# Scores of a chunked attention on TensorE: 12 products with a half-zero key operand replaced by 24 products over 64 rows each

## The chip, the core and the metric

The kernel runs on one core of a Trainium2 chip as one launch. The metric is the device time of that launch in microseconds (us). Engines are named as in the profile: PE is TensorE's matrix multiplication, PEld its weight loads, DVE is VectorE, ACT is ScalarE, POOL is GpSimd, SP is the queue from which nearly all transfers are issued.

## What is computed

Attention inside chunks of 64 tokens, then two MLPs, one after the other:

```python
q_c, k_c, v_c = ...            # B=8, H=8, S=576, D=64, in 9 chunks of 64 tokens
scores = scale * np.matmul(q_c, k_c.transpose(0, 1, 2, 4, 3))
scores = scores - np.max(scores, axis=-1, keepdims=True)
attn = np.exp(scores)
attn = attn / (np.sum(attn, axis=-1, keepdims=True) + 1e-09)
out = np.matmul(attn, v_c)
x = out.transpose(0, 2, 1, 3).reshape(4608, 512)
h = x @ w_in                                            # 512 -> 2048
x = (np.maximum(h, 0) + np.log1p(np.exp(-np.abs(h)))) @ w_out
h = np.maximum(np.maximum(x @ w1, x @ w2), x @ w3)      # 512 -> 768
out = h @ w_out2
```

## The kernel before

Tokens go in 9 blocks of 512. Products use a 4-byte type (`fp32r`) in which one product is not exact enough, so an operand is split into a high and a low part, and `PASS` runs three products (high by high, high by low, low by high) into one accumulator.

Attention works in 36 tiles: a tile is one block of 512 tokens by two heads, so that the two heads' 64 features fill 128 partitions. The first 8 tiles take a start-up path (`attention_first`). The other 28 take `attention`, which is spread between the steps of the first MLP: a step is `mlp1`, 12 products of 512 columns into `ph` (L743) and 12 into `acc` (L763).

One tile of `attention`: q and k are loaded and transposed on DVE (L633, L638) so that partitions 0 to 63 hold the features of one head and 64 to 127 those of the other. q is split into `Qh` (high and low, 128 x 512 each). k is split by `fill` into `kb`, two tiles of 128 x 1024 that hold, for each group of 32 tokens, the rows of head 0 with zeros beneath and then the rows of head 1 with zeros above; the zeros were written once by POOL (`zeros`, L1088). One product over all 128 rows, 128 query tokens by 256 key columns (L667), then gives the scores of both heads, which stand side by side in one accumulator bank. There are 4 groups of 128 tokens and 3 passes, so 12 products to a tile. The scores (`aps`, two banks, one buffer that the second product of the attention and other steps share) are copied to `p` by ACT and DVE in two copies of 64 x 512 (`copy_op`, L249 and L251), then come softmax on DVE and ACT, a transpose by way of DRAM, `fill` for the probabilities (`pb`) and 24 products with v (L720: weights of 64 columns, 128 moving columns).

The order of work on every engine comes from `Plan`: each operation carries a cost by engine (the scores `{"P": 1.31}`) and a due time, and a greedy list schedule fixes engine and order before the program is written. Buffers come from named pools (`places`); pool `z` has 4 slots of 128 x 2 x 512, which two key tiles and two probability tiles hold from the ninth tile on.

The second MLP follows (`mlp2`: L913, products of 256 columns, and L1024).

Of the kernel before, what the change touches and what calls it, by code (L numbers as in the profile page):

```python
# [20 lines left out]
P = 128  # L21
# [36 lines left out]
class Plan:  # L58
# [6 lines left out]
    def op(self, engs, fn, r=(), w=(), alloc=(), hold=(), after=(), due=None, lat=0.0, move=0.0):  # L65
        o = Op()
        o.move = move
        o.follow = o.start = None
        o.engs, o.fn, o.due, o.lat, o.allocs = engs, fn, due, lat, list(alloc)
        deps = dict.fromkeys(after)  # L70
        bufs = dict.fromkeys(o.allocs + list(hold))
        for item in r:
            b, key = item if isinstance(item, tuple) else (item, None)
            deps.update(dict.fromkeys(b.writers[key] if key in b.writers and key is not None else sum(b.writers.values(), [])))
            bufs[b] = None
        for item in w:
            b, key = item if isinstance(item, tuple) else (item, None)
            if key is None:
                deps.update(dict.fromkeys(sum(b.writers.values(), []) + sum(b.readers.values(), [])))
            else:  # L80
                deps.update(dict.fromkeys(b.writers.get(key, []) + b.readers.get(key, []) + b.readers.get(None, [])))
            bufs[b] = None
        for item in r:
            b, key = item if isinstance(item, tuple) else (item, None)
            b.readers.setdefault(key, []).append(o)
        for item in w:
            b, key = item if isinstance(item, tuple) else (item, None)
            b.writers[key] = [o]
        for b in bufs:
            if b.first is None:  # L90
                b.first = o
            else:
                deps[b.first] = None
        o.deps = list(deps)
        o.bufs = list(bufs)
        for b in o.bufs:
            b.uses += 1
        o.n = len(self.ops)
        self.ops.append(o)
        return o  # L100
# [78 lines left out]
def tile_kernel(ctx: ExitStack, tc: tile.TileContext, q, k, v, w_in, w_out, w1, w2, w3, wo2, out):  # L179
# [20 lines left out]
    def mem(kind, n, shape, dt, where=pool):  # L200
# [3 lines left out]

        "w": list(range(32)),
        "x": list(range(32, 40)),
        "z": list(range(40, 44)),
        "qh": [44],
        "vh": [45],
        "load": list(range(3)),  # L210
# [413 lines left out]
    def attention(t, after=()):  # L624
# [1 line left out]
        due_s, due_p = due_v - 2.0 * STEP, due_v - 1.4 * STEP  # L626
        Rq, Rk, Rv, Qh, Vh = Buf("rq"), Buf("rk"), Buf("rv"), slot("qh"), slot("vh")
        qT, kT = Buf("tmp"), Buf("tmp")
        kb, pb = big["k"], big["p"]
        loads(load_32(t, q, lambda: Rq.t), Rq, "q", 2.2, [Rq], after=after)  # L630
        loads(load_32(t, k, lambda: Rk.t), Rk, "k", 2.2, [Rk], after=after)
        loads(load_v(t, lambda: Rv.t), Rv, "v", 1.6, [Rv], after=after)
# [2 lines left out]
        tt_op(lambda: Qh.t[:, 1], lambda: qT.t, lambda: Qh.t[:, 0].bitcast(F32), ALU.subtract, [qT, (Qh, "h")], [(Qh, "l")])  # L635
        copy_op(lambda: Vh.t[:, 0], lambda: Rv.t, [Rv], [(Vh, "h")], alloc=[Vh])
        tt_op(lambda: Vh.t[:, 1], lambda: Rv.t, lambda: Vh.t[:, 0].bitcast(F32), ALU.subtract, [Rv, (Vh, "h")], [(Vh, "l")])
        op({"D": 0.69}, lambda e: nc.vector.transpose(kT.t, Rk.t), r=[Rk], w=[kT], alloc=[kT], after=last_p[-1:])  # L638

        def fill(dst, src, s):  # L640
            view = lambda l, e, r: dst[l].t.rearrange("p (u e s) -> p u e s", e=2, s=s)[r, :, e, :]
# [15 lines left out]
                )  # L657

        parts = lambda z: [(l, e) for l in z for e in range(2)]
        fill(kb, kT, 32)  # L660
        sc = Buf("aps")

        def do_s(e):
            o = sc.t.rearrange("p u (h f) -> p (u h) f", h=2)
            for h in range(HP):
                for n, (l, m) in enumerate(PASS):
                    nc.tensor.matmul(  # L667
                        o[:, h],
                        Qh.t[:, l, h * P:(h + 1) * P],
                        kb[m].t[:, 2 * h * P:2 * (h + 1) * P],  # L670
                        start=(n == 0),
                        stop=(n == 2),
                    )

        o = op({"P": 1.31}, do_s, r=[Qh] + parts(kb), w=[sc], alloc=[sc], after=last_t[-1:], due=due_s)
        last_s.append(o)

        pbuf = Buf("p")
        for c, r in enumerate(ROWS):
            copy_op(  # L680
                lambda r=r: pbuf.t[r].rearrange("p (a h i) -> p h a i", a=4, h=HP),
                lambda r=r, c=c: sc.t.rearrange("p u (h c a i) -> p (u h) c a i", c=2, a=4, i=32)[r, :, c],
                [sc],
                [(pbuf, c)],
                psum=True,
                alloc=[pbuf] if c == 0 else [],
            )
        softmax(
            pbuf,
            lambda red: pbuf.t.rearrange("p (b u i) -> p u b i" if red else "p (b u i) -> p b u i", b=2, i=32),  # L690
# [394 lines left out]
    def zeros(name, after):  # L1085
        big[name] = [slot("z", shape=[P, 2 * TB]) for _ in range(2)]
        for z in big[name]:
            op({"G": 0.9}, lambda e, z=z: nc.gpsimd.memset(z.t.bitcast(F32), 0.0), w=[(z, "z")], alloc=[z], after=after)  # L1088
# [12 lines left out]
    for n, (b, j, first, last) in enumerate(steps):  # L1101
        if n >= NJ and n % (NJ // HP) == 0:
            t = HP + n // (NJ // HP)
            if t < NTILE:
                if t == 2 * HP:
                    zeros("k", [done])
                    zeros("p", [done])
                attention(t, [first_loads[min(t, 11)]])
        h = mlp1(b, j, first, last)
        if b >= 2 and j in (0, 3, 6, 9) and len(store_early) < 4 * NJ2:  # L1110
            early(len(store_early), T0 + STEP * (n + 7), [h])
            store_early.append(h)
        if (b, j) == (NB - 1, 0):
            begun = [h]
# [40 lines left out]
```

## Time and profile before

| what | value |
|---|---|
| median of 3 runs (lowest to highest) | 1552.93 us (1551.62 to 1554.88) |
| the profiled execution's own time | 1553.11 us |
| its span, first to last instruction | 1551.4 us |
| PE busy | 1524.7 us, 98% |
| PEld busy | 1318.1 us, 85% |
| DVE busy | 963.3 us, 62% |
| ACT busy | 594.9 us, 38% |
| mean granted TensorE clock | 0.998 |

The span is what the profile covers; the 1.7 us between it and the execution's time lie outside the instructions. Busy time of PE is the time in which at least one product is in flight, and each product's record is longer than the distance to the next one's start. What a block of products costs is therefore read as the distance from its first start to the start of the block behind it.

### The profile page before, as it was taken

How to read it: one execution, taken by the hardware profiler on the slowest of the kernel's cores; microseconds unless marked ns; L12 is line 12 of the kernel's file. 1: busy time of each engine (PE TensorE's matmuls, PEld its weight loads, DVE VectorE, ACT ScalarE, POOL GpSimd, SP SyncE). 2: the span in 40 equal slices, each digit the busy share in tenths (PEclk: the TensorE clock that was granted, in tenths of full speed). 3: DMA queues.
4: the chain of work that ended last, by engine and by line, in shares of the span. 5: the costliest groups of instructions: out<-in, count | busy, mean ns of one | idle time of the engine just before them, and what ended most of it. 6: DMA issues, size and time to landing. Idle time of an engine off the chain costs nothing.

```text
span 1551.4 us, 23011 instructions
## 1 busy us (share of the span) xinstructions
PE 1524.7 (98%) x8930; PEld 1318.1 (85%) x8930; DVE 963.3 (62%) x1834; ACT 594.9 (38%) x1122; POOL 11.7 (1%) x19
## 2 busy tenths in 40 slices
PE   6999999999999999999999999999999999999998
PEld 5777888788888888888888888999999999999997
DVE  7988876866767766767676455553544545545443
ACT  5754344443444334433343343332322323323221
POOL 2000000000000000000000000000000000000000
PEclk9999999999999999999999999999999999999999
DMA  9354134543434425334342221222322122222121
GB/s 251 116 149 122 57 89 105 142 106 85 128 89 103 99 53 140 75 103 102 69 122 69 80 83 48 75 82 71 107 82 82 69 82 102 76 82 102 53 77 69
DMA packets 235214, 147.28 MB, mean 95 GB/s; under 512 B 167009, under 2 KB 202849, under 8 KB 235105
## 3 DMA queue, kind: packets, MB, share of 16 engines
q1 hardware_dynamic: 231904, 144.24, 32.4%
q10 hardware_dynamic: 3200, 1.57, 0.5%
q8 instruction: 70, 1.15, 0.3%
q14 instruction: 40, 0.32, 0.1%
HBM read 109.58 MB, written 36.18 MB: 94 GB/s over the span
## 4 chain that ended last, share of the span: by engine, by line
PE 94%; DVE 4%; DMA 1%; ACT 0%; issue 0%; ACTq 0%; DVEq 0%
PE acc L763 26%; PE ph L743 25%; PE ph L913 13%; PE aps L913 12%; PE acc L1024 10%; DVE tmp L256 3%; PE aps L720 3%; PE aps L667 3%; DMA s<-in_q_dram 1%; PE acc L557 1%; PE acc L606 1%; PE ph L369 1%; PE acc L526 0%; ACT s L249 0%; DVE s L256 0%
## 5 line engine op out<-in xcount | busy, mean ns | idle before, releaser
L763 PE MATMUL acc<-g,s 128*128 128x512 f32 x1728 | 427.7, 397 | 0.0
L743 PE MATMUL ph<-s,s 128*128 128x512 f32 x1728 | 420.0, 392 | 1.2 <-DVE s L256 0.9
L763 PEld LDWEIGHTS acc<-g,s 128*128 128x128 f32 x1728 | 323.4, 188 | 76.9 <-issue 1.0
L743 PEld LDWEIGHTS ph<-s,s 128*128 128x128 f32 x1728 | 321.6, 188 | 72.8 <-DVE s L256 1.2
L256 DVE TENSOR_TENSOR tmp<-aps,tmp 128x256 f32<-128x256 f32 x241 | 99.4, 422 | 280.8 <-PE aps L913 221.5
L913 PE MATMUL ph<-s,s 128*128 128x256 f32 x1944 | 267.6, 283 | 0.0
L913 PEld LDWEIGHTS ph<-s,s 128*128 128x128 f32 x1944 | 251.7, 191 | 4.5
L249 ACT COPY tmp<-ph 128x256 f32<-128x256 f32 x268 | 99.7, 372 | 349.9 <-PE ph L913 348.8
L256 DVE TENSOR_TENSOR g<-tmp,g 128x512 fp32r<-128x512 f32 x198 | 133.9, 687 | 149.9 <-ACT g L249 148.9
L753 ACT ACTIVATE tmp<-ph 128x512 f32<-128x512 f32 x144 | 86.3, 599 | 316.9 <-PE ph L743 312.5
L913 PE MATMUL aps<-s,s 128*128 128x256 f32 x1458 | 203.9, 285 | 3.6
L913 PEld LDWEIGHTS aps<-s,s 128*128 128x128 f32 x1458 | 186.0, 191 | 9.0 <-DVE tmp L256 8.8
L1024 PE MATMUL acc<-s,g 128*128 128x512 f32 x648 | 161.4, 398 | 1.9 <-ACT g L249 1.9
L256 DVE TENSOR_TENSOR s<-tmp,s 64x512 fp32r<-64x512 f32 (+1 forms) x212 | 142.2, 674 | 26.6 <-ACT s L249 22.7
L1024 PEld LDWEIGHTS acc<-s,g 128*128 128x128 f32 x648 | 119.7, 191 | 27.3 <-ACT g L249 2.2
L249 ACT CAST s<-tmp 128x512 fp32r<-128x512 f32 (+2 forms) x190 | 115.1, 609 | 67.4 <-DVE tmp L638 26.6
L249 ACT CAST g<-tmp 128x512 fp32r<-128x512 f32 x192 | 119.1, 620 | 28.3 <-PE acc L763 17.3
L256 DVE TENSOR_TENSOR tmp<-tmp,tmp 128x256 f32<-128x256 f32 (+1 forms) x152 | 83.1, 547 | 3.9
L249 ACT COPY p<-aps 64x512 f32<-64x512 f32 x50 | 29.1, 582 | 68.8 <-PE aps L667 52.8
L249 ACT COPY tmp<-acc 128x512 f32<-128x512 f32 (+1 forms) x66 | 37.3, 588 | 34.2 <-PE acc L1024 17.0
L720 PEld LDWEIGHTS aps<-s,s 128*64 128x64 f32 x672 | 44.5, 135 | 3.8
L667 PEld LDWEIGHTS aps<-s,s 128*128 128x128 f32 x336 | 43.8, 189 | 2.6
(97 smaller groups left out, 957.4 us busy)
## 6 DMA issues: line engine op xcount, KB each, us to landing
s<-wo2d SPq DMA_DIRECT2D x54, 512.0 KB, 3.3
s<-in_moe_w_out_dram SPq DMA_DIRECT2D x22, 512.0 KB, 4.9
x2d<-tmp SPq DMA_DIRECT2D x36, 256.0 KB, 2.8
s<-in_moe_w_dram SPq DMA_DIRECT2D x18, 512.0 KB, 4.2
s<-x2d SPq DMA_DIRECT2D x18, 512.0 KB, 4.6
s<-in_moe_w_in_dram SPq DMA_DIRECT2D x16, 512.0 KB, 4.9
out_dram<-tmp SPq DMA_DIRECT2D x29, 256.0 KB, 4.4
pd<-tmp SPq DMA_DIRECT2D x28, 256.0 KB, 2.1
```

The lines of the kernel that those rows point to most:

```text
L249: nc.scalar.copy(dst(), src())
L256: return op({"D": 0.69 * n}, lambda e: nc.vector.tensor_tensor(dst(), a(), b(), f), r=r, w=w, **kw)
L369: nc.tensor.matmul(o, ident, a.t, start=False, stop=False)
L557: nc.tensor.matmul(o[:, h], qT()[:, h * P:(h + 1) * P], blk[0]()[:, 2 * h:2 * h + 2].rearrange("p u e s -> p (u e s)"), start=True, stop=True,
L606: nc.tensor.matmul(o[:CH, c], rv()[:, c * CH:(c + 1) * CH], blk[1]()[:, c].rearrange("p e s -> p (e s)"), start=True, stop=True,)
L667: nc.tensor.matmul(o[:, h], Qh.t[:, l, h * P:(h + 1) * P], kb[m].t[:, 2 * h * P:2 * (h + 1) * P], start=(n == 0), stop=(n == 2),)
L720: nc.tensor.matmul(o[:CH, c], Vh.t[:, l, c * CH:(c + 1) * CH], z[m][:, c % 2, c // 4, c // 2 % 2], start=(n == 0), stop=(n == 2),)
L743: nc.tensor.matmul(ph.t, w[:, wi, kk * P:(kk + 1) * P], x[kk].t[:, xi], start=(kk == 0 and wi == 0 and xi == 0), stop=(kk == KD - 1 and wi ...
L753: in_line("y", op({"A": 0.6}, lambda e: nc.scalar.activation(l.t, ph.t, AF.Softplus), r=[ph], w=[l], alloc=[l]))
L763: nc.tensor.matmul(acc[m // 2].t[:, m % 2], w[:, wi, m * P:(m + 1) * P], g.t[:, gi, :], start=(first and wi == 0 and gi == 0), stop=(last ...
L913: nc.tensor.matmul(dst(), ws.t[:, wi, col + kk * P:col + (kk + 1) * P], x.t[:, xi, kk * HT:(kk + 1) * HT], start=(first and kk == 0 and wi ...
L1024: nc.tensor.matmul(acc[t // 2].t[:, t % 2], g.t[:, gi, t * P:(t + 1) * P], wo.t[:, wi], start=(j == 0 and wi == 0 and gi == 0), stop=(j == ...
```

## The change

The scores of a tile become 24 products of 64 rows (one head each), 128 query tokens by 128 key columns. Head 0 uses partitions 0 to 63 and writes the first bank of `aps`, head 1 partitions 64 to 127 and the second bank, and the two take turns. k is split like q, dense, into one tile `Kh` of pool `z` (one copy and one subtraction of 128 x 512 in place of two copies and two subtractions of 64 x 512). The key tiles with zeros and their two memsets go, and pool `z` has 3 slots. The scores leave `aps` in four copies of 64 x 256. The cost that the planner has for the scores stays at 1.31.

```diff
-        "z": list(range(40, 44)),
+        "z": list(range(40, 43)),
...
-        kb, pb = big["k"], big["p"]
+        Kh, pb = slot("z"), big["p"]
...
-        op({"D": 0.69}, lambda e: nc.vector.transpose(kT.t, Rk.t), r=[Rk], w=[kT], alloc=[kT], after=last_p[-1:])
+        op({"D": 0.69}, lambda e: nc.vector.transpose(kT.t, Rk.t), r=[Rk], w=[kT], alloc=[kT, Kh], after=last_p[-1:])
+        cut_up(Kh, lambda: kT.t, [kT])
...
-        fill(kb, kT, 32)
         sc = Buf("aps")
 
         def do_s(e):
-            o = sc.t.rearrange("p u (h f) -> p (u h) f", h=2)
+
             for h in range(HP):
+                cols = slice(h * P, (h + 1) * P)
                 for n, (l, m) in enumerate(PASS):
-                    nc.tensor.matmul(
-                        o[:, h],
-                        Qh.t[:, l, h * P:(h + 1) * P],
-                        kb[m].t[:, 2 * h * P:2 * (h + 1) * P],
-                        start=(n == 0),
-                        stop=(n == 2),
-                    )
-
-        o = op({"P": 1.31}, do_s, r=[Qh] + parts(kb), w=[sc], alloc=[sc], after=last_t[-1:], due=due_s)
+                    for u, r in enumerate(ROWS):
+                        nc.tensor.matmul(
+                            sc.t[:, u, cols], Qh.t[r, l, cols], Kh.t[r, m, cols], start=(n == 0), stop=(n == 2)
+                        )
+
+        o = op({"P": 1.31}, do_s, r=[Qh] + parts_of(Kh), w=[sc], alloc=[sc], after=last_t[-1:], due=due_s)
         last_s.append(o)
 
         pbuf = Buf("p")
         for c, r in enumerate(ROWS):
-            copy_op(
-                lambda r=r: pbuf.t[r].rearrange("p (a h i) -> p h a i", a=4, h=HP),
-                lambda r=r, c=c: sc.t.rearrange("p u (h c a i) -> p (u h) c a i", c=2, a=4, i=32)[r, :, c],
-                [sc],
-                [(pbuf, c)],
-                psum=True,
-                alloc=[pbuf] if c == 0 else [],
-            )
+            for u in range(2):
+                copy_op(
+                    lambda r=r, u=u: pbuf.t[r].rearrange("p (b u h i) -> p u h b i", b=2, u=2, h=HP)[:, u],
+                    lambda r=r, c=c, u=u: sc.t.rearrange("p u (h c b i) -> p u h c b i", c=2, b=2, i=32)[r, u, :, c],
+                    [sc],
+                    [(pbuf, (c, u))],
+                    psum=True,
+                    n=0.7,
+                    alloc=[pbuf] if c == 0 and u == 0 else [],
+                )
...
-                    zeros("k", [done])
                     zeros("p", [done])
```

PE before, at the first tile that takes this path. `aps_87` is the accumulator of the scores, `s_95` and `s_99` are the key tiles with zeros (high and low), `s_76` is q; `ph` and `acc` rows belong to the first MLP.

```order
L743 MATMUL ph_86<-s_46_529,s_87_1297 128x512 x3
L667 MATMUL aps_87<-s_95_1485,s_76_1078 128x256
L667 MATMUL aps_87<-s_99_1585,s_76_1078 128x256
L667 MATMUL aps_87<-s_95_1485,s_76_1078 128x256 x2
L667 MATMUL aps_87<-s_99_1585,s_76_1078 128x256
L667 MATMUL aps_87<-s_95_1485,s_76_1078 128x256 x2
L667 MATMUL aps_87<-s_99_1585,s_76_1078 128x256
L667 MATMUL aps_87<-s_95_1485,s_76_1078 128x256 x2
L667 MATMUL aps_87<-s_99_1585,s_76_1078 128x256
L667 MATMUL aps_87<-s_95_1485,s_76_1078 128x256
L763 MATMUL acc_89<-g_65,s_80_1186 128x512 x6
```

PE of the change at the same tile; `s_87_1258` is now k, dense, high and low in one tile.

```order
L743 MATMUL ph_85<-s_46_529,s_65_929 128x512 x3
L763 MATMUL acc_89<-g_63,s_57_801 128x512 x6
L763 MATMUL acc_88<-g_63,s_57_801 128x512 x6
L669 MATMUL aps_87<-s_87_1258,s_76_1078 128x128 x24
L743 MATMUL ph_86<-s_27_348,s_69_979 128x512 x3
```

Twelve products of 256 columns became 24 of 128 columns, and the first tile's block moved several steps forward (it stood behind the step with weights `s_87_1297`, and stands now ahead of the step with `s_69_979`); it no longer waits for POOL's zeros.

DVE of the change at that tile: the transpose of k, the low part of a step's `g`, and the low part of k.

```order
L638 STREAM_TRANSPOSE tmp_73<-rk_76 128x512
L256 TENSOR_TENSOR tmp_74<-tmp_74,s_85_1237 128x512
L256 TENSOR_TENSOR g_64<-tmp_72,g_64 128x512
L256 TENSOR_TENSOR s_87_1258<-tmp_73,s_87_1258 128x512
L312 TENSOR_SCALAR tmp_67<-tmp_67 128x512
```

DVE before at a later tile, where the key operand was filled half by half (`s_95` high, `s_99` low, 64 rows each).

```order
L638 STREAM_TRANSPOSE tmp_71<-rk_76 128x512
L256 TENSOR_TENSOR s_106_1868<-rv_77,s_106_1868 128x512
L251 CAST s_95_1485<-tmp_71 64x16x32
L256 TENSOR_TENSOR s_107_1884<-aps_87,s_107_1884 64x512
L256 TENSOR_TENSOR s_99_1585<-tmp_71,s_95_1485 64x16x32 x2
```

Two subtractions over 64 partitions became one over 128, and the one stands, at the first tile, behind the low part of the step that PE runs just ahead of the scores.

## Rows read from the trace of the kernel before

**Rows 1.** The page: busy time of each engine, and the shares of the chain that ended last by engine and line.

```profile
PE 1524.7 (98%) x8930; PEld 1318.1 (85%) x8930; DVE 963.3 (62%) x1834; ACT 594.9 (38%) x1122; POOL 11.7 (1%) x19
...
PE 94%; DVE 4%; DMA 1%; ACT 0%; issue 0%; ACTq 0%; DVEq 0%
PE acc L763 26%; PE ph L743 25%; PE ph L913 13%; PE aps L913 12%; PE acc L1024 10%; DVE tmp L256 3%; PE aps L720 3%; PE aps L667 3%; DMA s<-in_q_dram 1%; PE acc L557 1%; PE acc L606 1%; PE ph L369 1%; PE acc L526 0%; ACT s L249 0%; DVE s L256 0%
```

**Rows 2.** Busy time of each engine by stretches; the stretch is given in us from the span's start, with its length, then busy us and number of instructions. PEclk is the granted clock.

```profile
core 0: us, PE busy (x) PEld busy (x) DVE busy (x) ACT busy (x) POOL busy (x), PEclk, DMA share, GB/s
120.00:180.00 60.00, 60.00 (x253) 47.25 (x252) 49.16 (x101) 23.62 (x41) 0.96 (x1) 1.00 0.37 106
400.00:600.00 200.00, 200.00 (x1041) 165.94 (x1040) 141.09 (x249) 80.08 (x136) 0.00 (x0) 1.00 0.38 97
600.00:800.00 200.00, 200.00 (x1047) 166.06 (x1045) 139.93 (x247) 80.28 (x136) 0.00 (x0) 1.00 0.38 95
800.00:880.00 80.00, 80.00 (x429) 66.26 (x428) 48.09 (x85) 29.68 (x50) 0.00 (x0) 1.00 0.26 76
```

**Rows 3.** Groups of instructions by line and shape: partitions x elements of the output (and weights' rows*columns for PE), count, then busy us, mean ns of one, and idle time ahead of the group with what ended it.

```profile
L720 PE MATMUL aps<-s,s 128*64 128x128 f32 x672 | 44.9, 223 | 0.0
L720 PEld LDWEIGHTS aps<-s,s 128*64 128x64 f32 x672 | 44.5, 135 | 3.8
L667 PE MATMUL aps<-s,s 128*128 128x256 f32 x336 | 44.5, 282 | 0.0
L667 PEld LDWEIGHTS aps<-s,s 128*128 128x128 f32 x336 | 43.8, 189 | 2.6
```

**Rows 4.** PE in order of time, 215 to 232 us: start, length of the merged piece, line, output, weights' rows*columns, output shape, count.

```profile
217.25 2.97 PE L763 MATMUL acc<-g,s 128*128 128x512 f32 x12
220.06 1.60 PE L720 MATMUL aps<-s,s 128*64 128x128 f32 x24
221.50 2.96 PE L743 MATMUL ph<-s,s 128*128 128x512 f32 x12
224.30 2.98 PE L763 MATMUL acc<-g,s 128*128 128x512 f32 x12
227.11 1.59 PE L667 MATMUL aps<-s,s 128*128 128x256 f32 x12
228.54 2.91 PE L743 MATMUL ph<-s,s 128*128 128x512 f32 x12
```

**Rows 5.** All engines in order of time from 227.08 to 227.12 us, the place where a block of scores begins.

```profile
226.88 0.40 PE L763 MATMUL acc<-g,s 128*128 128x512 f32 x1
226.89 0.61 SPq L408 DMA_DIRECT2D rk<-in_k_dram  x1
227.11 0.28 PE L667 MATMUL aps<-s,s 128*128 128x256 f32 x1
227.12 0.19 PEld L667 LDWEIGHTS aps<-s,s 128*128 128x128 f32 x1
```

**Rows 6.** PEld alone at that place (227.04 to 227.10 us).

```profile
226.88 0.19 PEld L667 LDWEIGHTS aps<-s,s 128*128 128x128 f32 x1
```

**Rows 7.** PEld alone from 221.46 to 221.50 us, where a block with 64 weight columns (L720) ends and a block with 128 (L743) begins.

```profile
221.38 0.13 PEld L720 LDWEIGHTS aps<-s,s 128*64 128x64 f32 x1
221.44 0.19 PEld L743 LDWEIGHTS ph<-s,s 128*128 128x128 f32 x1
```

**Rows 8.** All engines from 221.64 to 221.70 us, just behind that.

```profile
221.44 0.22 PE L720 MATMUL aps<-s,s 128*64 128x128 f32 x1
221.50 0.44 PE L743 MATMUL ph<-s,s 128*128 128x512 f32 x1
221.55 0.19 PEld L743 LDWEIGHTS ph<-s,s 128*128 128x128 f32 x1
```

**Rows 9.** L743 by itself: count, then shortest, median and longest ns.

```profile
L743 PEld LDWEIGHTS ph<-s,s x1728: 186/188/192, 56.3 to 965.2; 128*128 128x128 f32 x192
L743 PE MATMUL ph<-s,s x1728: 387/389/503, 56.3 to 965.4; 128*128 128x512 f32 x192
```

**Rows 10.** Groups on DVE and ACT that the change touches, or that are nearest to what it adds, columns as in the third group.

```profile
L256 DVE TENSOR_TENSOR s<-tmp,s 64x512 fp32r<-64x512 f32 x112 | 76.6, 684 | 10.5 <-ACT s L249 7.7
L256 DVE TENSOR_TENSOR s<-tmp,s 128x512 fp32r<-128x512 f32 x91 | 62.2, 688 | 11.3 <-ACT s L249 10.1
L249 ACT CAST s<-tmp 128x512 fp32r<-128x512 f32 x110 | 67.8, 620 | 35.9 <-DVE tmp L256 20.3 <-DVE tmp L317 15.1
L249 ACT CAST s<-tmp 64x512 fp32r<-64x512 f32 x71 | 43.9, 618 | 30.1 <-DVE tmp L638 26.6 <-POOL s L1088 1.9 <-DMA tmp<-pd 0.7
L249 ACT COPY p<-aps 64x512 f32<-64x512 f32 x50 | 29.1, 582 | 68.8 <-PE aps L667 52.8 <-DVE tmp L256 14.9 <-DVE g L256 0.8
L249 ACT COPY tmp<-ph 128x256 f32<-128x256 f32 x268 | 99.7, 372 | 349.9 <-PE ph L913 348.8
L753 ACT ACTIVATE tmp<-ph 128x512 f32<-128x512 f32 x144 | 86.3, 599 | 316.9 <-PE ph L743 312.5 <-DVE s L326 2.5 <-DMA tmp<-pd 1.5
```

**Rows 11.** Who waited for whom: the waits of PE by themselves, and one of PEld; us in total, times, longest us.

```profile
PE acc L1024 <- ACT g L249: 1.9, 1, 1.9
PE ph L368 <- ACT s L249: 1.2, 1, 1.2
PE ph L743 <- DVE s L256: 0.9, 1, 0.9
...
PEld aps L913 <- DVE tmp L256: 8.8, 26, 0.3
```

## The prediction

> **What bounds the kernel now.** The first view to read is the page's busy time and its last chain: PE is busy for 1524.7 of 1551.4 us, and the chain that ended last is PE for 94% [rows 1]. The stretches say that this holds where the change is made: from 400 to 880 us PE is busy for all of the time at a granted clock of 1.00 (the 2.4 GHz level), while DVE and ACT are busy for about 70% and 40% [rows 2]. PE waits hardly anywhere behind the start-up: its longest waits there are 0.9 to 1.9 us, once each [rows 11]. So in the stage of the change one microsecond of PE is one microsecond of the kernel, and DVE and ACT count only where PE waits for them.
>
> Next, what a block of scores costs PE. Mean durations (282 ns a product) don't say it, since products overlap. Distances between starts do: a block of scores starts at 227.11 and the next block at 228.54, 1.43 us for 12 products of 256 columns, 0.119 us each. The block with v, 24 products of 128 columns with 64 weight columns, goes from 220.06 to 221.50, 1.44 us, 0.060 us each [rows 4]. Count over 12 gives the tiles: 336 / 12 = 28 [rows 3], so all scores cost 28 x 1.43 = 40.0 us, which is the chain's 3% for L667 [rows 1].
>
> Then, what sets these distances. Each product loads its own weights. A load of 128 columns takes 189 ns and one of 64 columns 135 ns [rows 3]: 54 ns for 64 columns, so the streaming part of a full load is about 0.107 us, the rest fixed latency. In steady state it is hidden: the load of the scores' first weights starts at 226.88, together with the product ahead of it, and is long done at 227.11; the second load starts at 227.12, right behind the start of the first product [rows 5, 6]. It shows where the cover is too short. When the block with v ends, the load for L743 starts at 221.44, its product at 221.50, only 0.06 us later, and that product is recorded with 0.44 us where the median is 0.389 [rows 7 to 9]: it stood still for 0.05 us, until its weights were in, 0.11 us after the load began. And the next load starts at 221.55, 0.11 us behind the first, though its product had begun at 221.50. So weights of 128 columns come at one in 0.11 us at best over the same rows. A 256-column product (0.119 us) hides that; a 128-column product (0.060 us) doesn't.
>
> **The change, part by part.** *Scores.* Now 12 loads and 12 x 256 columns; then 24 loads of 64 rows x 128 columns, each with 128 moving columns. The moving columns are 3072 in both, so if nothing ran side by side the columns alone would be 24 x 0.060 = 1.44 us, as now. What can change the time is whether the two heads, in disjoint halves of the array's rows, run side by side, and then the loads decide, since 128 weight columns in 0.11 us stand against 0.060 us of moving columns. All products of the trace, like those in [rows 3, 4], have 128 rows (the first number of their form), so this is bounded from both sides:
> - two loads side by side, and the two products under them: a pair takes one load, 0.107 to 0.119 us (the upper end is what a pair's worth of columns takes now). 12 x 0.110 = 1.32 us, and 1.28 to 1.43 at the ends. The last product's exit is in it, since the following block's first load takes the place of a 13th.
> - loads one behind another: 24 x 0.110 = 2.64 us, 2.57 to 2.86 at the ends.
>
> I take the first, at 0.110: the array already overlaps a load with the product ahead [rows 5], the heads share no partition, and they write different banks. 1.43 - 1.32 = 0.11 us a tile, 28 tiles, **-3.1 us**; ends -4.2 and 0.
>
> The Trainium skill, TensorEngine Tiling (Array Packing), Key Properties, says that different tiles can execute weight loads and products in parallel; no run here shows it yet. By that rule the sum is the one just made. The Trainium skill, TensorE: Matmul & The Clock Gate, LDWEIGHTS, says that a load goes by its columns and not by its rows; by it, too, half the rows don't make a load shorter.
>
> *k.* Out go two casts of 64 x 512 (618 ns on ACT) and two subtractions (684 ns on DVE), in come one cast (620) and one subtraction (688) of 128 x 512 [rows 10], since these take the same over 64 and 128 partitions. That is 0.62 us of ACT and 0.68 of DVE less per tile, hidden under PE's columns: 0. The two memsets on POOL go: 0.
>
> *Copies of the scores.* Two of 64 x 512 at 582 ns become four of 64 x 256; the nearest row is 372 ns for 256 columns, on ACT [rows 10]: 1.49 for 1.16 us. Three of four stand on ACT, so the softmax starts some 0.3 us later at most and `aps` is held so much longer. The next user of `aps` is steps away (a step is 5.6 us): 0.
>
> *Place in the order.* The block of the first tile moves forward, and there its key's low part stands on DVE behind the low part of `g` of the step just done. From the end of that step's `ph`: activation 0.60, two casts of 0.62 on ACT (`g`, then k), one subtraction 0.69 on DVE, 2.5 us and the hand-overs; cover is one block of L763, 2.81 us [rows 4, 10]. Cost 0, at most 0.5 us, once. PE is fully busy there now [rows 2].
>
> *Pool z with 3 slots.* In the second MLP the splits of x draw on it; PE's only repeated wait there is 0.3 us, 26 times, for DVE's sums [rows 11], not for a buffer: 0.
>
> Sum: the profiled execution's 1553.1 us - 3.1 = **1550.0 us**. That execution lies 0.2 us above the median of the runs shown, so it can stand for it. With the ends and 1 us for waits, this case's own range is 1548.5 to 1554.
>
> **The rivals.**
> 1. *Loads one behind another* (slower). Place: the 28 blocks; price 2.64 - 1.43 = +1.21 us a tile, +33.9 us, **1587 us** (2.57 to 2.86: 1585 to 1593). It decides as soon as a pair takes over 0.119 us, that is when the second head's load begins more than 9 ns behind the first's; 18 ns behind is 0.2% of the kernel. For it: loads start 0.11 us apart at 221.44 and 221.55 although the product between was already under way [rows 7, 8]. Against it: those two go to the same rows, where the second has to wait in any case.
> 2. *Loads half covered*: the second load starts some way behind the first (0.13 to 0.17 us a pair, between the two): 1.56 to 2.04 us a block, +0.13 to +0.61, **1557 to 1570 us**. Nothing in the trace sets a point here.
> 3. *Changing the row layout empties the array.* A product's record is 0.40 us long where the distance is 0.23 [rows 4, 5], so about 0.16 us of results would be awaited at the block's start and the load (0.11) laid bare; the same at its end: about 0.5 us a tile, +14 us on the forecast, **1564 us**. Against it: at 217.25 to 224.30 the form of the weights changes from 128 to 64 columns and back, at a cost of those 0.05 us alone [rows 4, 7, 8]. The Trainium skill, TensorEngine Tiling (Array Packing), Key Properties, states the rule that a change of tiling mode drains the engine. By that rule this rival would be the forecast; the trace doesn't bear it out for columns, and has no row for rows.
> 4. *A load of 64 rows takes half as long* and the pairs run at 0.060 us: 0.72 us a block, -0.71 x 28 = -19.9, **1533 us**. No row has a shorter load for other than fewer columns.
> 5. *Nothing runs side by side and loads are hidden nonetheless*: 1.44 us, no change. Rows 7 to 9 speak against it.
>
> **How the numbers follow.** About 0.2% (3.1 us) is what a measurement of this kernel can tell from no change, so the forecast stands at that edge. Chances: forecast 0.42, rival 1 0.30, rival 2 0.14, rival 3 0.06, rival 4 0.07, rival 5 0.01. Faster: 0.45 of the forecast's 0.42 (below 1549.8) and rival 4, 0.26. Same: the rest of the forecast and rival 5, with a little of rival 2's near end, 0.26. Slower: rivals 1, 3 and most of 2, 0.48. For 8 in 10 the range takes the forecast's 0.42 with its low end, rivals 2 and 3 (0.20) and two thirds of rival 1 (0.20): **1548.5 to 1590 us**; rival 4 and the far end of rival 1 are left out.
>
> **What would show it.** In the profile after, the distance from the first score product to the next block, now 1.43 us: 1.3 to 1.4 bears the forecast out, 2.6 or more rival 1, 0.7 rival 4. The starts of the two heads' loads: together, or 0.11 us apart. A gap between the last L763 product and the first score product, and after the last: rival 3. PE idle under 1 us at the first tile, and 100% busy from 400 to 880 us; if PE waits there for `p`, `Kh` or `aps`, the parts that I cost at nothing were wrong. ACT and DVE busy lower by about 8 us (28 x 0.3 us) and 19 us.

## The result, and the profile after

The change makes the kernel slower: 1561.55 us (median of 4 runs, 1561.01 to 1563.39) against 1552.95 us for the kernel before (4 runs), a ratio of 1.0056 with the interval [1.0043, 1.0069]. The forecast was 1550.0 us, a gain of 3 us; the kernel lost 8.6. The time lies inside the range, but the forecast went the wrong way, and the nearest case is rival 3 (1564 us), to which I had given 6 in 100.

The page of the changed kernel, which answers to [rows 1]: busy us, share of the span, instructions.

```profile
PE 1530.9 (98%) x9266; PEld 1315.5 (84%) x9266; DVE 944.2 (61%) x1813; ACT 584.8 (37%) x1143; POOL 9.8 (1%) x17
```

DVE and ACT lost 19.1 and 10.1 us, about as forecast (19 and 8), and it bought nothing: PE is still what bounds the kernel. The stretch of PE in which all changed work lies can be read off the line L743 by itself, which answers to [rows 9]: shortest, median and longest ns, then the first and the last start.

```profile
L743 PE MATMUL ph<-s,s x1728: 387/389/793, 55.5 to 975.3; 128*128 128x512 f32 x192
```

From the first L743 product to the last are 975.3 - 55.5 = 919.8 us; before 965.4 - 56.3 = 909.1 [rows 9]. So **+10.7 us** came into this stage. The stretch ahead of it is 0.8 us shorter and the one behind it 1.3 (1560.0 - 975.3 = 584.7 against 586.0), which makes the 8.6 us between the spans. In the last 14 us the granted clock is 0.97, and was 0.84 in the last 15 us before; neither end holds any work of the scores. Of the change only pool `z` reaches into the second MLP, and PE's one long wait there is 1.9 us as before [rows 11].

**A block of scores.** PE of the changed kernel in order of time, 396 to 405 us, columns as in [rows 4]. In both kernels 23 of the 28 blocks stand like this one, between L763 and L743.

```profile
396.30 2.97 PE L763 MATMUL acc<-g,s 128*128 128x512 f32 x12
399.21 1.56 PE L669 MATMUL aps<-s,s 64*128 64x128 f32 x24
400.69 3.00 PE L743 MATMUL ph<-s,s 128*128 128x512 f32 x12
403.53 1.60 PE L720 MATMUL aps<-s,s 128*64 128x128 f32 x24
```

Read the distances from start to start, and beside them those of the block at 227.11 in [rows 4], which has the same neighbours. The block of scores takes 400.69 - 399.21 = 1.48 us (1.49 at most of the 28), and took 1.43. But its neighbours are longer too: L763 ahead of it takes 2.91 us and took 2.81, L743 behind it 2.84 and took 2.74. All three together take 7.23 us and took 6.98; over the 23 blocks the means are 7.23 and 6.99. That is **0.24 us a tile, 28 x 0.24 = +6.7 us**, of which only 0.06 us a tile shows in the distance that the prediction had named as its test.

Why the neighbours are longer is seen closer by, here at a block with L743 ahead and L763 behind: PE and PEld at the first pair, then at the end (a merged piece is given as start, length and count).

```profile
326.88 0.39 PE L743 MATMUL ph<-s,s 128*128 128x512 f32 x1
327.20 0.19 PEld L669 LDWEIGHTS aps<-s,s 64*128 64x128 f32 x2 [0.35 <-DVE tmp L323]
327.20 0.33 PE L669 MATMUL aps<-s,s 64*128 64x128 f32 x2
...
327.20 0.30 PEld L669 LDWEIGHTS aps<-s,s 64*128 64x128 f32 x4 [0.35 <-DVE tmp L323]
...
328.42 0.19 PEld L669 LDWEIGHTS aps<-s,s 64*128 64x128 f32 x2
...
328.69 0.19 PEld L763 LDWEIGHTS acc<-g,s 128*128 128x128 f32 x1
328.69 0.51 PE L763 MATMUL acc<-g,s 128*128 128x512 f32 x1
```

The pairs do what the forecast said. Two loads together last 0.19 us, as one does; four last 0.30, so the second pair comes 0.11 us behind the first; the two products of the first pair last 0.33 together. What went wrong stands at both ends. Before, the first load of a block ran under the product ahead of it, 0.23 us early [rows 5, 6]. Now the first two loads start only at 327.20, with their own products, and PEld sat idle for 0.35 us ahead of them. At the end, L763's first load starts at 328.69, with its product again and 0.27 us behind the loads ahead of it (328.42), where a pair follows a pair by 0.11. That product is recorded with 0.51 us, against a median of 0.389 for such products [rows 9]: 0.12 us in which it stood still until its weights were in. So at each change between products of 64 and of 128 rows the first load doesn't run under the products ahead but starts with its own product, and that product comes late: 0.32 us behind the last one of L743 (326.88), where such products follow each other by 0.23 us [rows 4]. These are the gaps that the prediction had named as rival 3's sign.

The Trainium skill, TensorEngine Tiling (Array Packing), Key Properties, says that a change of tiling mode drains the engine and that different tiles load and multiply in parallel. For the change of rows this trace agrees with both: the bare loads at 327.20 and 328.69, and the two loads that together last 0.19 us.

**The sixth block.** The rest of the 10.7 us, 4.0, stands at one place. PE after, 279 to 297 us, with two rows of DVE from there; the brackets hold the idle time ahead and what ended it.

```profile
279.32 1.61 PE L720 MATMUL aps<-s,s 128*64 128x128 f32 x24
284.95 1.97 PE L669 MATMUL aps<-s,s 64*128 64x128 f32 x24 [4.02 <-DVE s L256]
286.85 9.59 PE L743 MATMUL ph<-s,s 128*128 128x512 f32 x36
296.28 1.60 PE L720 MATMUL aps<-s,s 128*64 128x128 f32 x24
...
283.50 0.67 DVE L256 TENSOR_TENSOR s<-tmp,s 128x512 fp32r<-128x512 f32 x1
284.21 0.68 DVE L256 TENSOR_TENSOR s<-aps,s 64x512 fp32r<-64x512 f32 x1
```

PE of the kernel before at the same place:

```profile
278.90 1.61 PE L720 MATMUL aps<-s,s 128*64 128x128 f32 x24
280.35 2.28 PE L743 MATMUL ph<-s,s 128*128 128x512 f32 x9
282.94 0.50 PE L743 MATMUL ph<-s,s 128*128 128x512 f32 x1 [0.30 <-ACT s L249]
284.35 6.19 PE L743 MATMUL ph<-s,s 128*128 128x512 f32 x26 [0.91 <-DVE s L256]
290.38 1.60 PE L720 MATMUL aps<-s,s 128*64 128x128 f32 x24
```

Before, three L743 blocks followed L720 there and waited 0.30 and 0.91 us, for the high and the low part of their operand. After, the list schedule put the scores directly behind L720. Both write `aps`, of which there is one buffer, so the scores had to wait until all of L720's result was split out of it: the last subtraction that reads `aps` runs from 284.21 to 284.89, and the scores start at 284.95. The low part of k was in at 284.17, so it was `aps` that they waited for last. The clock then comes on top. Busy time by stretches, columns as in [rows 2]:

```profile
279.30:284.90 5.60, 1.63 (x25) 1.47 (x23) 5.49 (x9) 2.29 (x4) 0.00 (x0) 1.00 0.51 140
284.90:286.90 2.00, 1.95 (x25) 1.83 (x25) 1.91 (x3) 0.00 (x0) 0.00 (x0) 0.76 0.27 57
286.90:288.90 2.00, 2.00 (x7) 1.61 (x6) 1.24 (x3) 1.00 (x3) 0.00 (x0) 0.50 0.56 142
288.90:291.00 2.10, 2.10 (x10) 1.72 (x9) 1.80 (x4) 0.00 (x0) 0.00 (x0) 0.90 0.48 93
```

DVE is busy for 5.49 of the 5.60 us: here it is the bound. Behind the idle time the granted clock falls to 0.76 and then to 0.50 (the 1.2 GHz level), and comes back by 291 us. From L720 at 279.32 to the next at 296.28 are 16.96 us; without waits the same blocks take 1.44 + 0.09 (L720, longer ahead of the scores) + 1.49 + 2.84 + 2 x 2.74 (L743) = 11.34, so 5.6 us are lost. Before it is 290.38 - 278.90 = 11.48 against 1.44 + 2.80 + 2 x 2.74 = 9.72 (2.80 for L743 right behind L720 [rows 4]), 1.8 lost. The net 3.9 us and the 6.7 above make 10.6 of the 10.7 us that the stage lost.

### The profile page after: what moved, and what is told of

It reads as the page before. It is cut to its first block, busy times and chain, and to the rows that moved or that the text cites. A ratio compares the mean times of both kernels' runs of the same rounds, so it can differ in the third digit from the quotient of the medians.

```text
span 1560.0 us, 23657 instructions
## 1 busy us (share of the span) xinstructions
PE 1530.9 (98%) x9266; PEld 1315.5 (84%) x9266; DVE 944.2 (61%) x1813; ACT 584.8 (37%) x1143; POOL 9.8 (1%) x17
## 4 chain that ended last, share of the span: by engine, by line
PE 93%; DVE 4%; DMA 1%; ACT 0%; SPq 0%; issue 0%; ACTq 0%; DVEq 0%
PE ph L743 26%; PE acc L763 25%; PE ph L913 13%; PE aps L913 12%; PE acc L1024 10%; DVE tmp L256 3%; PE aps L669 3%; PE aps L720 2%; DMA s<-in_q_dram 1%; PE acc L557 1%; PE acc L606 1%; PE ph L369 1%; DVE s L256 0%; PE acc L526 0%; ACT s L249 0%
## 5 line engine op out<-in xcount | busy, mean ns | idle before, releaser
L763 PE MATMUL acc<-g,s 128*128 128x512 f32 x1728 | 428.4, 397 | 0.0
L743 PE MATMUL ph<-s,s 128*128 128x512 f32 x1728 | 422.6, 394 | 0.0
L763 PEld LDWEIGHTS acc<-g,s 128*128 128x128 f32 x1728 | 323.3, 188 | 77.4 <-issue 1.0
L743 PEld LDWEIGHTS ph<-s,s 128*128 128x128 f32 x1728 | 322.3, 188 | 72.8 <-issue 0.5
L913 PEld LDWEIGHTS aps<-s,s 128*128 128x128 f32 x1458 | 186.0, 191 | 9.0 <-DVE tmp L256 8.8
L256 DVE TENSOR_TENSOR s<-tmp,s 128x512 fp32r<-128x512 f32 (+2 forms) x184 | 123.0, 673 | 42.2 <-ACT s L249 39.5
L249 ACT CAST s<-tmp 128x512 fp32r<-128x512 f32 (+2 forms) x169 | 101.8, 608 | 58.6 <-DVE tmp L638 24.0
L249 ACT COPY p<-aps 64x256 f32<-64x256 f32 x87 | 28.9, 367 | 78.5 <-PE aps L669 67.1
L669 PEld LDWEIGHTS aps<-s,s 64*128 64x128 f32 x672 | 40.0, 189 | 14.0 <-issue 6.2
L669 PE MATMUL aps<-s,s 64*128 64x128 f32 x672 | 44.0, 278 | 4.0 <-DVE s L256 4.0
```

The lines of the kernel that those rows point to most:

```text
L249: nc.scalar.copy(dst(), src())
L256: return op({"D": 0.69 * n}, lambda e: nc.vector.tensor_tensor(dst(), a(), b(), f), r=r, w=w, **kw)
L669: nc.tensor.matmul(sc.t[:, u, cols], Qh.t[r, l, cols], Kh.t[r, m, cols], start=(n == 0), stop=(n == 2))
L743: nc.tensor.matmul(ph.t, w[:, wi, kk * P:(kk + 1) * P], x[kk].t[:, xi], start=(kk == 0 and wi == 0 and xi == 0), stop=(kk == KD - 1 and wi ...
L763: nc.tensor.matmul(acc[m // 2].t[:, m % 2], w[:, wi, m * P:(m + 1) * P], g.t[:, gi, :], start=(first and wi == 0 and gi == 0), stop=(last ...
L913: nc.tensor.matmul(dst(), ws.t[:, wi, col + kk * P:col + (kk + 1) * P], x.t[:, xi, kk * HT:(kk + 1) * HT], start=(first and kk == 0 and wi ...
```

## The experiments

Each starts from the changed kernel, except the last. The kernel before took 1553.54 us (13 runs) on the chip of the first four, 1551.13 (5 runs) on that of the next four and 1553.55 (13 runs) on that of the last; ratios are to these. To set the runs against each other I use the stage as above, from the first to the last start of the `ph` products: 909.1 us before, 919.8 after. The changed kernel itself was not run again on these chips, so whole times are set against its 1561.55 us with that reserve.

**The place of the sixth block.** The scores of that tile are put behind the first step of a later block.

```diff
-        o = op({"P": 1.31}, do_s, ..., alloc=[sc], after=last_t[-1:], due=due_s)
+        o = op({"P": 1.31}, do_s, ..., alloc=[sc], after=[*last_t[-1:], *behind], due=due_s)
...
-                attention(t, [first_loads[min(t, 11)]])
+                attention(t, [first_loads[min(t, 11)]], [hs[32]] if t == 13 else [])
```

> The changed kernel, with the scores of one tile alone (the sixth of the 28, whose block stood still for 4.0 us at 280.7 us) put behind the first step of the third token block in PE's order. Theory A (the loss is in two parts: about 0.26 us at each of 28 blocks, from changing between products of 128 rows and of 64 rows, and one stall from the new order): the stall goes back to about what the kernel before has there (1.65 us), the 0.7 us of lower clock behind it goes too, so about 3 us less than the changed kernel, 1558.5 us; the 28 blocks keep their 1.49 us. Theory B (the whole loss sits in the 28 blocks and the stall only takes the place of the earlier one): within 0.5 us of 1561.5 us.

Measured: 1560.98 us (1559.75 to 1561.91), 1.0052 [1.0036, 1.0069]. That is 0.6 us below the changed kernel with overlapping ranges: nearer to theory B's number than to A's, and no gain that these runs can tell. PE in order of time:

```profile
285.24 0.50 PE L743 MATMUL ph<-s,s 128*128 128x512 f32 x1 [0.81 <-ACT s L249]
...
292.99 1.60 PE L720 MATMUL aps<-s,s 128*64 128x128 f32 x23 [0.81 <-DVE s L256]
...
387.21 1.56 PE L669 MATMUL aps<-s,s 64*128 64x128 f32 x24 [0.63 <-DVE s L256]
```

The wait of 4.0 us is gone and the clock with it, but the schedule laid smaller waits elsewhere, and the stage is 917.5 us: 2.3 us of the 3.9 came back there, and the stretch ahead of the stage was 1.4 us longer in this execution. The place explains part of the loss and is not the larger part.

**Products over all 128 rows.** The scores become 12 products of 128 rows and 128 columns, which changes what they compute: the two heads are summed.

```diff
-                    for u, r in enumerate(ROWS):
-                        nc.tensor.matmul(
-                            sc.t[:, u, cols], Qh.t[r, l, cols], Kh.t[r, m, cols], start=(n == 0), stop=(n == 2)
-                        )
+                    nc.tensor.matmul(
+                        sc.t[:, n // 2, cols], Qh.t[:, l, cols], Kh.t[:, m, cols], start=(n != 1), stop=(n != 0)
+                    )
```

> Scores by 12 products of all 128 rows with 128 columns (k dense, both heads' rows in one product, the third pass into the other bank). It leaves out that the two heads are kept apart and that the three passes are added, so the scores are not the reference's; everything around it is the changed kernel's. It has the same loads at the same distance as a pair of 64-row products, and no change of row layout. Theory A (changing the row layout costs about 0.35 us a block, the pairs themselves 0.111 us): a block of 12 x 0.108 = 1.30 us with nothing at its ends but 0.05 us at the exit, so 0.40 us a tile less than the changed kernel, 28 tiles 11 us: about 1550.5 us. Theory B (a product of 128 columns loses its time because loads come at 0.145 us for such a pair, whatever the rows): about the same as the changed kernel, 1561 us.

Measured: 1556.3 us (10 runs, 1554.77 to 1557.74), 1.002 [1.0011, 1.003]. PE around a block:

```profile
394.60 2.98 PE L762 MATMUL acc<-g,s 128*128 128x512 f32 x12
397.41 1.45 PE L668 MATMUL aps<-s,s 128*128 128x128 f32 x12
398.70 2.96 PE L742 MATMUL ph<-s,s 128*128 128x512 f32 x12
401.50 1.60 PE L719 MATMUL aps<-s,s 128*64 128x128 f32 x24
```

As many loads in a row as there are pairs, the same number of columns under them, one layout throughout: 2.81 ahead, 1.29 for the block, 2.80 behind, 6.90 us together against 7.23 in the changed kernel. The difference of **0.33 us a tile** is the price of the layout, in and out. Over 28 tiles it is 9.2 us; the stage is 911.7 us, 8.1 below the changed kernel. The order of work is the same and so the wait at the sixth block is there too (4.0 us, for DVE), but the block behind it takes 2.6 us at the lower clock, and that place is 0.8 us longer than in the changed kernel: 27 x 0.33 - 0.8 = 8.1. The whole is 5.8 us above A's number. Some 3 us of that lie in the stage (A had 0.40 us for all 28 tiles); the rest lies outside it or between executions, and I don't place it.

**One more full product, ahead of the pairs or between them.** Two kernels, with one added product of 128 rows and 128 columns a tile, overwritten by what follows: `start` has it ahead of the first pair (`h == 0`), `mid` in the middle of the block (`h == 2`).

```diff
             for h in range(HP):
                 cols = slice(h * P, (h + 1) * P)
+                if h == 0:     # 2 in the second kernel
+                    nc.tensor.matmul(sc.t[:, 0, cols], Qh.t[:, 0, cols], Kh.t[:, 0, cols], start=True, stop=True)
```

> The changed kernel with one product of 128 rows and 128 columns more, ahead of each block of 24; what it writes is overwritten by the first real product. Control for the next kernel. Theory A (a change of row layout costs about 0.1 us of emptying and 0.11 us of bare load, each way): the added product moves the change behind itself: about 0.06 us a tile, +1.6 us, 1563 us. Theory B (no cost of changing): one load more, 0.11 us a tile, +3 us, 1564.5 us.

> The same one product of 128 rows, now in the middle of each block of 24, between the second and the third group of 128 tokens: two changes of row layout more for each tile, no product more than the kernel with it at the start. Theory A: the gap around it is 2 x 0.264 us where 0.111 would be, +0.42 us a tile over the changed kernel, +11.7 us, 1573 us, and 10 us over the kernel with the product at the start. Theory B: the same as with the product at the start.

Measured: `start` 1566.37 us (1565.89 to 1569.2), 1.0091 [1.0076, 1.0106]; `mid` 1576.54 us (1575.85 to 1578.78), 1.0155 [1.014, 1.017]. PE of `start`:

```profile
326.78 2.92 PE L745 MATMUL ph<-s,s 128*128 128x512 f32 x12
329.54 0.22 PE L668 MATMUL aps<-s,s 128*128 128x128 f32 x1
329.69 1.56 PE L671 MATMUL aps<-s,s 64*128 64x128 f32 x24
331.17 3.06 PE L765 MATMUL acc<-g,s 128*128 128x512 f32 x12
334.07 2.91 PE L745 MATMUL ph<-s,s 128*128 128x512 f32 x12
```

PE of `mid`, then PEld at its added product:

```profile
328.67 2.92 PE L745 MATMUL ph<-s,s 128*128 128x512 f32 x12
331.52 0.89 PE L671 MATMUL aps<-s,s 64*128 64x128 f32 x12
332.34 0.33 PE L668 MATMUL aps<-s,s 128*128 128x128 f32 x1
332.60 0.89 PE L671 MATMUL aps<-s,s 64*128 64x128 f32 x12
333.41 3.07 PE L765 MATMUL acc<-g,s 128*128 128x512 f32 x12
336.32 2.92 PE L745 MATMUL ph<-s,s 128*128 128x512 f32 x12
...
332.34 0.19 PEld L668 LDWEIGHTS aps<-s,s 128*128 128x128 f32 x1
```

In `start` the L745 block ahead takes 2.76 us, where it takes 2.85 in `mid`: the loss moved with the border, from in front of the added product to behind it, where the short product now takes 0.15 us until the first pair. In `mid` the same product makes two borders more. From the first product of the scores to L765 are 333.41 - 331.52 = 1.89 us, against 1.49 in the changed kernel: the product and the two borders cost 0.40 us. With the blocks ahead and behind, a tile of `mid` takes 2.85 + 1.89 + 2.91 = 7.65 us, one of `start` 2.76 + 1.63 + 2.90 = 7.29: 0.36 us, and 0.34 (7.65 and 7.31) at the 23 blocks between L765 and L745. 28 x 0.34 = 9.5, the two stages are 10.8 us apart (932.3 and 921.5), and the 1.3 more stands at the sixth block, which runs at the lower clock. The whole times are 10.2 us apart, as theory A had it. The same work in a different place, at the price of one more change in and out: this decides for the border, against an effect of the pairs themselves. It also decides against a wait for a semaphore at the first load, which the block's outer borders have: the two inner borders lie within `do_s`, where nothing is waited for, and still the added product's load starts only with its product (332.34). Both whole times lie above theory A's (1563 and 1573 us) by some 3.5 us. The stage of `start` is only 1.7 us longer than that of the changed kernel, so the rest of its 4.8 lies outside: in its profiled execution, the longest of the four, ahead of the stage, where the granted clock in the first 60 us was 0.91 against 0.97, and behind it.

**The order of the heads, and the block twice.** `seq` runs all products of head 0 and then all of head 1; `twice` runs the 24 products two times.

```diff
 seq:
-            for h in range(HP):
-                cols = slice(h * P, (h + 1) * P)
-                for n, (l, m) in enumerate(PASS):
-                    for u, r in enumerate(ROWS):
+            for u, r in enumerate(ROWS):
+                for h in range(HP):
+                    cols = slice(h * P, (h + 1) * P)
+                    for n, (l, m) in enumerate(PASS):
 twice:
-            for h in range(HP):
+            for h in [*range(HP), *range(HP)]:
```

> The changed kernel with the 24 products of a tile in another order: the 12 of head 0 first, then the 12 of head 1, in place of the two heads in turn. Theory A (two loads run side by side because they go to different rows; over the same rows one load comes in 0.111 us): 24 x 0.111 = 2.66 us where the changed kernel has 12 x 0.111 = 1.34, +1.33 us a tile, +37 us, 1598.5 us. Theory B (a load of 64 rows is simply half as long, and turns don't matter): 1561.5 us.

> The changed kernel with each tile's 24 products run twice in a row (the second time writes the same scores again). No change of row layout more. Theory A (a pair costs 0.111 us, the rest of a block's cost sits at its two ends): +12 x 0.111 = 1.34 us a tile, +37.5 us, 1599 us. Theory B (the loss of the 28 blocks is spread over the pairs, 0.145 us each): +1.74 us a tile, +49 us, 1610 us.

Measured: `seq` 1590.32 us (2 runs), 1.0254 [1.0224, 1.0284]; `twice` 1601.15 us (2 runs), 1.0324 [1.0294, 1.0354]. PE of `seq`, then products of its scores by themselves in the first 0.95 us and the rest of the block (length, PE busy and count, PEld busy and count, PEclk):

```profile
334.16 2.51 PE L669 MATMUL aps<-s,s 64*128 64x128 f32 x24
336.60 3.07 PE L763 MATMUL acc<-g,s 128*128 128x512 f32 x12
...
334.15:335.10 0.95, 0.94 (x8) 0.94 (x9) 1.00 0.03 6
335.10:336.60 1.50, 1.50 (x18) 1.42 (x17) 1.00 0.00 0
```

PE of `twice`:

```profile
336.29 2.90 PE L669 MATMUL aps<-s,s 64*128 64x128 f32 x48
339.12 3.08 PE L763 MATMUL acc<-g,s 128*128 128x512 f32 x12
```

`twice` came within about 2 us of theory A's 1599 and gives the price of the pairs without the ends: 2.83 - 1.49 = 1.34 us for 12 more pairs, **0.112 us a pair**. It also says that the ends, 1.49 - 1.34 = 0.15 us within the block, don't grow with it. `seq` was expected at 1598.5 by the theory that one head alone goes at the pace of a pair. It does: 8 products in the first 0.95 us, one in 0.12. But the block takes 2.44 us, not 24 x 0.112 + 0.15 = 2.84: at least 16 products lie in the remaining 1.50 us (one behind another there would be 13), so the second head had begun while the last products of the first were still to come. This overlap takes 28 x 0.40 = 11 us off; the whole time missed the theory's by 8, and I don't place the other 3. Taking turns is thus worth 28 x 0.95 = 27 us, and what makes it so is that two loads over disjoint rows go side by side.

**Size of the weights and of the moving operand.** `narrow` loads 64 weight columns instead of 128 (half of the queries' scores are left out), `wide` moves 256 columns instead of 128 (neighbouring groups' scores too, overwritten).

```diff
 narrow:
-                            sc.t[:, u, cols], Qh.t[r, l, cols], Kh.t[r, m, cols], ...
+                            sc.t[:CH, u, cols], Qh.t[r, l, h * P:h * P + CH], Kh.t[r, m, cols], ...
 wide:
+                wide = slice(min(h, 2) * P, (min(h, 2) + 2) * P)
...
-                            sc.t[:, u, cols], Qh.t[r, l, cols], Kh.t[r, m, cols], ...
+                            sc.t[:, u, wide], Qh.t[r, l, cols], Kh.t[r, m, wide], ...
```

> The changed kernel with weights of 64 columns (the first 64 of each 128 query tokens) in place of 128, the moving side as it is. It leaves out the scores of every second chunk, whose place takes a copy of the first's. Theory A (a pair's 0.111 us is the load of 128 weight columns, and 64 take half of it): 0.060 us a pair, set by its 128 moving columns, -0.61 us a tile, -17 us, 1544 us. Theory B (the 0.111 us is something else of a pair of 64-row products): 1561.5 us.

> The changed kernel with 256 moving columns in each of the 24 products in place of 128, the weights as they are. The products of neighbouring groups overwrite each other, so these are not the reference's scores. Theory A (not only the loads of the two heads but their products too run side by side): 0.120 us a pair, as a product of 256 columns takes now, +0.1 us a tile, +3 us, 1564.5 us. Theory B (only the loads overlap, the moving columns of the two heads go one behind the other, which 2 x 0.060 us in a pair of 0.111 nearly allows): 0.24 us a pair, +1.5 us a tile, +43 us, 1604 us.

Measured: `narrow` 1545.96 us (4 runs), 0.9968 [0.9948, 0.9987]; `wide` 1566.59 us (2 runs), 1.0101 [1.0071, 1.013]. PE of `narrow`:

```profile
324.24 0.93 PE L669 MATMUL aps<-s,s 64*64 64x128 f32 x24
325.10 3.07 PE L763 MATMUL acc<-g,s 128*128 128x512 f32 x12
```

PE of `wide`:

```profile
328.24 1.70 PE L670 MATMUL aps<-s,s 64*128 64x256 f32 x24
329.87 3.07 PE L764 MATMUL acc<-g,s 128*128 128x512 f32 x12
```

Half the weight columns: 0.86 us, less 0.15 for the ends 0.71, 0.059 us a pair, and a whole time 2 us from theory A's 1544. So the load set the 0.112, as the forecast had it. Twice the moving columns: 1.63 us, less 0.15 1.48, 0.123 us a pair, hardly more. So the products of the two heads run side by side as well; one behind another, a pair of 256 columns would need 2 x 0.119 [rows 4].

**The four copies alone.** The kernel before with its two copies of 64 x 512 split into four of 64 x 256.

```diff
         for c, r in enumerate(ROWS):
-            copy_op( ... p h a i ... [r, :, c] ... )
+            for u in range(2):
+                hs = slice(2 * u, 2 * u + 2)
+                copy_op( ... p h a i ... [:, hs] ... [r, hs, c] ... n=0.7 ... )
```

> The kernel before, with one part of the change alone: its scores leave the accumulator in four copies of 64 x 256 in place of two of 64 x 512. Theory A (the copies are hidden under PE, as costed at nothing): within 1.5 us of the kernel before. Theory B (later scores hold the accumulator or the softmax up and PE waits): PE would have to wait 0.3 us at each of 28 tiles, +8.5 us.

Measured: 1550.87 us (10 runs, 1550.14 to 1552.9), 0.9986 [0.9976, 0.9996]: 0.14% faster than the kernel before, and so than both. That is 2.7 us below it, more than the 1.5 that theory A allowed, but on the side away from theory B: the copies cost nothing. PE at the place where the other two kernels wait:

```profile
276.93 3.02 PE L766 MATMUL acc<-g,s 128*128 128x512 f32 x12
279.78 8.36 PE L746 MATMUL ph<-s,s 128*128 128x512 f32 x36
```

The schedule, given other costs for the copies, put a block of L766 between the attention's block with v and the three blocks (L746 here) that stood right behind it before and had to wait; PE goes on from the one to the others without a gap. The stage is 907.4 us, 1.7 below that of the kernel before, which is about what that kernel lost at this place. The gain is the order's, not the copies'.

## Why the prediction was wrong

- **Pairs at 0.110 us: right.** Loads and products of the two heads start together and a pair takes 0.112 us (`twice`, and the pieces of 0.19 and 0.30 us above). 12 x 0.112 = 1.34 us, not 1.32, is 0.09 us under the 1.43 of before: -2.5 us of the forecast's -3.1. `full`, which has the same loads without borders, takes the same 0.09 us a tile less than the kernel before (6.90 against 6.99). Rivals 1, 2 and 5 fall by this, and rival 4 with it: half the rows don't shorten a load, half the columns do (`narrow`).
- **Rival 3, argued away: this is the step that failed.** I had the mechanism, and its working was close: 0.5 us a tile against the 0.33 of `full` and the 0.34 of `mid`. I set it aside because the change from 128 to 64 weight columns costs only 0.05 us. That row says nothing of rows: the load of L743 behind L720 still starts under the products ahead of it [rows 7], and the load behind the scores does not. Within the block 0.15 us, ahead of it 0.09, behind it 0.09 make the 0.33, 28 x 0.33 = +9.2 us, three times the 3.1 that the pairs were to give back. That this rival's 1564 us comes so near the measured 1561.55 is in part luck: it had 14 us for the borders, and nothing for the sixth block.
- **"The last product's exit is in it": wrong.** It holds only if the next block's first load can stand under the last pair. The test that I named, the distance from the first score product to the next block, would have shown 1.49 and so 0.06 us of the 0.24; most of the loss is booked on the neighbours.
- **Place in the order, at most 0.5 us: mis-sized.** I looked at the first tile alone, where PE indeed doesn't wait. The sixth tile's block moved too, to directly behind L720, and I had written that the next user of `aps` is steps away. There it is the next block: 4.0 us of waiting and a lower clock behind it, some 3.9 us more than the kernel before lost at that place.
- **k, copies, pool z at nothing: right.** The changed kernel's only wait of the scores beyond the start-up is that one, and `four` shows the copies alone without a loss. The savings of DVE and ACT were hidden, as said.

The sum of what was found, in profiled executions: -2.5 (pairs) + 9.2 (borders) + 3.9 (the sixth block) - 2.0 (outside the stage, which varies) = +8.6 us, and 1561.79 - 1553.11 = 8.7. The borders are shown by `full` and `mid`; the sixth block is read from the trace, and `late` gave back only part of it, because the schedule made new waits.

## What to carry to other kernels

Products over part of the rows run side by side, but each passage between them and products over all rows costs some 0.15 to 0.2 us, so they pay only in runs long enough: here a block of 12 pairs saved 0.09 us and paid 0.33. By these numbers a run nearly four times as long would have broken even, an estimate that no run tested. When a short block is replaced, read the start of the first load and the length of the neighbours too, not only the block. When a list schedule is run anew, go through every place where a moved block follows another user of its buffer, not only the first one.

## What the runs showed of the hardware

- A change of rows and a change of columns are not alike: 128 to 64 weight columns and back leaves the next load under the products ahead (0.06 us early, [rows 7, 8]), 128 rows to 64 and 64 to 128 don't (load and product both at 327.20, and both at 328.69).
- Two products of 64 rows and 256 moving columns run in about 0.12 us together, as long as one of 128 rows takes (0.119 [rows 4]); with 64 weight columns a pair of 128 moving columns takes 0.059 us. Two heads side by side take the time of one, once the ends are paid.
- One head's products in a row don't hold back the other head's behind them in program order: in `seq` the second head began about 0.95 us into the block, with products of the first still to come.
- An idle time of 4.0 us on PE was followed by a granted clock of 0.76, 0.50 and 0.90 in three stretches of 2 us. At that place 5.6 us were lost in all, so some 1.6 beside the wait.
